# Another order of the first units in a recurrence-and-MLP kernel: unit 1's first scan directly behind its gates, weight conversions and weight sums at other places

## The chip, the cores and the metric

The kernel runs on one core of a Trainium2 chip. The metric is the device time of an execution in microseconds (us). A profiled execution has a span, from its first to its last instruction, and a time that is a little longer than the span.

## The reference

Two blocks follow each other. The first is a recurrence over 768 tokens, for 4 batches and 8 heads of width 48, with a gate for every channel; the second normalises the result and passes it through an MLP with a residual.

```python
f = 1.0 / (1.0 + np.exp(-f_logit))
for t in range(S):
    state = f[:, :, t, :, None] * state + np.einsum('bhd,bhe->bhde', k[:, :, t], v[:, :, t])
    y[:, :, t] = np.einsum('bhd,bhde->bhe', q[:, :, t], state)
...
xn = (x - mu) / np.sqrt(var + 1e-06) * g_ln
ch = np.maximum(xn @ w_ch1, 0.0) @ w_ch2
return x + ch
```

Here x is y with its heads side by side (384 columns), w_ch1 is 384 x 1536 and w_ch2 is 1536 x 384. The weights come as 64-bit floating-point numbers; the kernel computes in 32 bits.

## The kernel before

The 768 tokens are cut into 12 units of 64 tokens, each with all 4 batches. A unit passes through two chains of stages.

The first is the attention of unit n, written `a{n}.stage`. `gates` transposes f_logit on TensorE (only in units 0 to 2; later units get their transposed inputs by DMA) and takes the sigmoid on ScalarE. `after` and `upto` are two scans on VectorE, the products of gates behind and up to each token (lines 669 and 681). `kx` transposes k, and `k` and `q` multiply k and q by the scans. `scores` multiplies q and k on TensorE into the PSUM tile `shared`, and `causal` masks the product on VectorE. `carried` (with the state of the unit before) and `values` fill the tile `py`. `kt` transposes k back, `chunk` and `state` bring the state forward, with `kept` in between. `stats` are means and variances (VectorE, and for `rstd` GpSimd), `norm` makes xn, and `turn` transposes xn to xt on TensorE and ScalarE. In unit 0 most stages are done in two halves, whose names end in 0 and 1.

The second chain is the MLP, `m{n}`: a step is one group of matmuls. `ph` is the first layer with a relu on ScalarE, `po` and `pp` are the second. For unit 0 the first layer is done in halves by the steps `h00` and `h01` (line 901); unit 1 and unit 2 use line 1023, and from unit 3 on the first layer works with fewer products on sums of weights (the tiles `v`, line 612), and from unit 2 on the second layer does so too (the tiles `mixed`, line 586).

The weights come in 12 pieces of 768 KB. `f` fetches a piece, `r` reads it on ScalarE (two conversions, `upper` and `units`), `w` writes it (three VectorE operations, the first on `body`, the last on `upper`, and one addition on GpSimd, line 563). `u` and `U` make one of the sums of w1 on VectorE or GpSimd, `t` and `T` four differences of w2. `l` and `L` load an input of a unit on SP's or ScalarE's DMA queue (`l2f` is f_logit of unit 2, a last digit is a half); `p`, `P` and `x` split an input into planes (a copy on ScalarE), write them out on GpSimd's or SP's queue, and read them back transposed. `d` is a matmul whose result nobody uses, and which only keeps TensorE busy.

Nothing schedules this work at run time or at build time. The first units stand in a list of such words, START, and the rest in a list UNIT, repeated for each unit. The function `run` takes a list word by word, and each word writes its instructions at the end of the queues of its engines; an engine takes its queue in order. The tile framework adds the waits. PSUM has four single banks that are used in rotation (`one_bank`), so a matmul group also waits until the reader of the group four before it is done.

```python
            elif kind in "lL":
                queues = (nc.scalar if kind == "L" else nc.sync,)
...
                {"r": read, "w": write, "f": fetch, "t": mix, "d": idle,
                 "T": lambda: mix(nc.gpsimd), "u": mix_step,
                 "U": lambda: mix_step(nc.gpsimd)}[token]()
```

Of the kernel before, what the change touches and what calls it, by code (L numbers as in the profile page):

```python
# [299 lines left out]


START = """
l0q0 L0f1 d d a0.carried d a0.gates0 d a0.after0 l0k0 a0.upto0 f a0.q0 a0.gates1 a0.kx0 l0k1 r
l0q1 a0.after1 f a0.kx1 a0.k0 a0.scores0 a0.upto1 w L0v1 a0.causal0 a0.k1 l0v0 a0.q1 r f
a0.scores1 a0.values0 r w f a0.kt a0.causal1 l1f a0.stats0 d w a0.values1 l1q a0.norm0 r d
a0.chunk a0.turn0 f a0.stats1 w a1.gates h00 h00 a0.norm1 f a0.turn1 r a1.after h00 a0.state
l2f h01 a1.upto w l1k h01 a1.kept f h01 h01 h00 a2.gates a1.q a1.kx a1.carried r l1v a1.k w f
a1.scores l3f a1.causal h00 r h01 a1.values a1.kt l2k f l2q w a1.stats r h01 a1.norm a1.chunk
P3f0 w h00 a1.turn a2.kx a2.after p3f1 a2.k r m1 m1 a2.upto f f l3k w a2.q r p3k0 x3f a1.state
m1 f a2.kept l4v P3k1 l2v m1 l3q r m1 m1 w x3k r a2.carried a3.gates w a2.scores w u U  # L310
a2.causal P3q1 m0 m0 a2.kt a3.after m0 U P3q0 L4f a2.values a3.k a2.stats L4k a2.chunk P4f1 m1
x3q m1 a2.state a3.upto p4f0 m0 l5f a2.norm U p3K1 u m0 a2.turn m0 P4k0 m1 P3K0 T a3.q x4f u u
P4k1 u a4.gates l4q u a3.kt a3.kept m2 m2 P5f0 m2 a3.carried l3v a4.after a3.scores m2 p4q0 x4k
m2 a4.upto u m2 u a3.causal p4q1 t m2 s2 a3.chunk a4.k t L5k a3.values a3.state x4q p5k0
a3.stats m1 m1 a3.norm P5f1 P4K1 m2 U m2 a4.q x5f m2 p5k1 l6f l5q m2 a4.kept m2 a3.turn y3 l5v
U m2 m1 p4K0 a5.gates
"""
UNIT = """
a{n}.kt a{n}.carried p{p}f1 a{o}.after a{n}.scores m{m} a{n}.causal m{m} m{m} m{m} P{o}q0 m{m}
# [874 lines left out]
```

## Time and profile before

| | |
|---|---|
| median of 3 runs | 430.95 us (430.91 to 432.98) |
| profiled execution | 431.19 us, span 429.4 us |
| mean granted clock of TensorE | 0.987 of full speed |
| TensorE (PE) busy | 414.6 us, 97% of the span |
| VectorE (DVE) busy | 335.2 us, 78% |
| ScalarE (ACT) busy | 214.2 us, 50% |
| GpSimd (POOL) busy | 120.7 us, 28% |

Each engine has one queue, and an engine is busy while it runs an instruction. Where one engine is busy all the time, the others matter only where it waits for them. The lines of the page and of the timelines are read in the prediction.

### The profile page before, as it was taken

To read this page: it belongs to the slowest core of one execution; us is meant where nothing else is said; L and a number is where in the kernel's file an instruction comes from. 1 tells how busy PE (TensorE), PEld (TensorE's weight loads), DVE (VectorE), ACT (ScalarE), POOL (GpSimd) and SP (SyncE) were. 2 spreads that over 40 slices of the span, in tenths; PEclk is the share of its full clock that TensorE was granted. 3 is DMA by queue.
4 is the path that set the end of the run, shared out by engine and by line. 5 is a ranking of instruction groups with operands and counts; after the bars stand their busy time and mean duration, and the time that the engine had idled before them with its cause. 6 is when DMAs were issued, how large, how long until landed. Compare 5 with 4: busy or idle time off the path is not lost.

```text
span 429.4 us, 12958 instructions
## 1 busy us (share of the span) xinstructions
PE 414.6 (97%) x5429; PEld 386.7 (90%) x5429; DVE 335.2 (78%) x539; ACT 214.2 (50%) x364; POOL 120.7 (28%) x148
## 2 busy tenths in 40 slices
PE   5699999999999999999999999999999999999995
PEld 3589988657879899999999999999999999999995
DVE  5998797795886779879879879879879879665561
ACT  2485856542553473573574573574574462351320
POOL 2362453561024116016016016016015014012021
PEclk9599999999999999999999999999999999999999
DMA  9998979886988797896898797797796781301001
GB/s 170 287 226 182 241 237 215 187 212 178 178 134 227 169 215 190 201 207 174 200 186 202 193 217 170 186 213 196 176 209 166 175 135 44 94 2 25 15 9 34
DMA packets 167647, 71.68 MB, mean 167 GB/s; under 512 B 151760, under 2 KB 157840, under 8 KB 167584
## 3 DMA queue, kind: packets, MB, share of 16 engines
q1 hardware_dynamic: 151728, 54.38, 60.1%
q0 software_dynamic: 3872, 12.64, 8.3%
q10 hardware_dynamic: 11984, 3.79, 4.2%
q8 instruction: 44, 0.72, 0.7%
q14 instruction: 19, 0.16, 0.1%
HBM read 28.31 MB, written 23.59 MB: 121 GB/s over the span
## 4 chain that ended last, share of the span: by engine, by line
PE 88%; ACT 3%; DVE 2%; SPq 2%; DMA 2%; issue 1%; POOL 0%; ACTq 0%; DVEq 0%; POOLq 0%
PE pp L1052 32%; PE bx L952 11%; PE by L952 10%; PE ph L1023 7%; PE po L1033 5%; PE bz L952 4%; PE ph L901 3%; PE py L808 2%; PE py L758 2%; PE shared L772 2%; PE bw L952 2%; PE bv L952 2%; SPq L475 2%; PE xp L887 2%; PE shared L846 2%; DMA kraw<-in_k_dram 1%
## 5 line engine op out<-in xcount | busy, mean ns | idle before, releaser
L963 ACT ACTIVATE h<-h 128x512 f32<-128x512 f32 x45 | 28.4, 630 | 44.1 <-DVE h L960 37.9
L1052 PE MATMUL pp<-mixed,h 128*128 128x192 f32 x240 | 42.4, 326 | 0.0
L1052 PE MATMUL pp<-w,h 128*128 128x192 f32 x240 | 40.8, 326 | 0.0
L1052 PE MATMUL pp<-mixed,s 128*128 128x192 f32 x240 | 40.6, 326 | 0.0
L1052 PEld LDWEIGHTS pp<-mixed,s 128*128 128x128 f32 x240 | 39.3, 190 | 0.0
L1052 PEld LDWEIGHTS pp<-w,h 128*128 128x128 f32 x240 | 38.9, 190 | 0.3
L1052 PEld LDWEIGHTS pp<-mixed,h 128*128 128x128 f32 x240 | 39.1, 190 | 0.1
L960 DVE TENSOR_TENSOR h<-h,bx 128x512 f32<-128x512 f32 x36 | 24.6, 683 | 17.1 <-PE bx L952 16.4
L889 ACT ACTIVATE xt<-xp,gain 128x128 f32<-128x128 f32 x72 | 20.0, 376 | 34.5 <-PE xp L887 34.5
L669 DVE TENSOR_TENSOR_SCAN after<-gates,ends 128x1040 f32<-128x1040 f32 (+1 forms) x13 | 29.8, 2290 | 6.0 <-ACT gates L700 3.2
L440 ACT COPY Kplanes<-kh 128x1024 uint16<-128x1024 uint16 x18 | 18.2, 1047 | 29.0 <-DVE kh L717 25.2
L441 POOL DMA_DIRECT2D qhalves<-qplanes x9 | 4.9, 545 | 98.4 <-ACT qplanes L440 98.4
L1033 PE MATMUL po<-w,h 128*128 128x384 f32 x96 | 32.3, 489 | 0.0
L1023 PE MATMUL ph<-xt,w 128*128 128x256 f32 x144 | 31.9, 380 | 0.2 <-ACT xt L889 0.2
L1023 PEld LDWEIGHTS ph<-xt,w 128*128 128x128 f32 x144 | 27.1, 190 | 4.3 <-ACT xt L889 0.5
L952 PE MATMUL bx<-y,v 128*128 128x128 f32 x216 | 28.7, 275 | 0.1
L681 DVE TENSOR_TENSOR_SCAN upto<-gates,starts 128x1040 f32<-128x1040 f32 (+1 forms) x13 | 28.1, 2158 | 0.5
L1033 PEld LDWEIGHTS po<-w,h 128*128 128x128 f32 x96 | 17.8, 190 | 11.3
L952 PEld LDWEIGHTS bx<-y,v 128*128 128x128 f32 x216 | 26.4, 192 | 0.1
L834 POOL TENSOR_SCALAR rstd<-mv 128x2 f32<-128x2 f32 (+1 forms) x13 | 8.1, 626 | 62.2 <-DVE mv L832 61.9
L440 ACT COPY kplanes<-kraw 128x1024 uint16<-128x1024 uint16 x18 | 18.3, 1047 | 9.1 <-DMA kraw<-in_k_dram 6.0
L563 POOL TENSOR_TENSOR w<-w_0upper,w_0units 128x768 int32<-128x768 int32 x7 | 14.6, 2082 | 28.6 <-DVE w_0upper L561 28.6
(172 smaller groups left out, 960.5 us busy)
## 6 DMA issues: line engine op xcount, KB each, us to landing
w_0words<-in_moe_w_ch_dram SPq DMA_DIRECT2D x7, 768.0 KB, 5.0
v<-in_v_dram SPq DMA_DIRECT2D x46, 96.0 KB, 4.0
Khalves<-Kplanes POOLq DMA_DIRECT2D x16, 256.0 KB, 3.6
kraw<-in_k_dram SPq DMA_DIRECT2D x40, 96.0 KB, 4.2
fhalves<-fplanes POOLq DMA_DIRECT2D x14, 256.0 KB, 3.8
kraw<-in_q_dram SPq DMA_DIRECT2D x36, 96.0 KB, 3.0
fraw<-in_f_logit_dram ACTq DMA_DIRECT2D x27, 96.0 KB, 3.0
khalves<-kplanes POOLq DMA_DIRECT2D x9, 256.0 KB, 3.6
```

The source lines that it names most:

```text
L440: nc.scalar.copy(out=to, in_=src)
L563: nc.gpsimd.tensor_tensor(out=to.bitcast(I32), in0=upper, in1=units, op=ALU.add)
L669: nc.vector.tensor_tensor_scan(out=at["after"].rearrange(flat)[:, c0:c1][:, ::-1], data0=gt[:, c0 + 1:c1 + 1][:, ::-1], data1=ends.rearran ...
L681: nc.vector.tensor_tensor_scan(out=at["upto"].rearrange(flat)[:, c0:c1], data0=gt[:, c0:c1], data1=starts.rearrange(flat)[:, c0:c1], initi ...
L889: nc.scalar.mul(out=xt[:, m, g * P:(g + 1) * P], in_=pt[:, m], mul=gain[:, m:m + 1])
L901: nc.tensor.matmul(ph[:, j], lhsT=w1[:, m, (i + j) * P:(i + j + 1) * P], rhs=xt[:, m, tokens], start=m == 0, stop=m == KD - 1)
L952: nc.tensor.matmul(banks[bank][:, i], lhsT=right[:, i * P:(i + 1) * P], rhs=left, start=new and i == 0, stop=True, skip_group_check=True)
L960: nc.vector.tensor_tensor(out=out[to], in0=out[to], in1=bank, op=op)
L963: nc.scalar.activation(out=out[to], in_=out[to] if bank is None else bank, func=AF.Relu)
L1023: nc.tensor.matmul(ph[:, j], lhsT=w1[:, m, (i + j) * P:(i + j + 1) * P], rhs=xt[:, m], start=m == 0, stop=m == KD - 1)
L1033: nc.tensor.matmul(po, lhsT=h[:, i, g * P:(g + 1) * P], rhs=w2[:, i], start=i == 0, stop=i == KF - 1)
L1052: nc.tensor.matmul(pp, lhsT=a[:, i], rhs=b[:, i], start=i == 0, stop=i == KH - 1)
```

## The change

Only START changes. It holds the same number of words before and after, 243, and the same stages and steps of the MLP. GpSimd makes one sum of w1 more than before, and VectorE one less. The other words of the table read like the lines shown. Of the loads and the writes of planes, several change their queue: `l0f1` and `l0v1`, halves of unit 0's f and v, go from ScalarE's queue to SP's; `L2f`, `L3q`, `L3v`, `L4q`, `L4v`, `L5v` and `L6f` come to ScalarE's from SP's, and `l4f` leaves it. The rest is order.

```diff
 START = """
...
-a0.chunk a0.turn0 f a0.stats1 w a1.gates h00 h00 a0.norm1 f a0.turn1 r a1.after h00 a0.state
-l2f h01 a1.upto w l1k h01 a1.kept f h01 h01 h00 a2.gates a1.q a1.kx a1.carried r l1v a1.k w f
...
+a0.chunk a0.state a0.turn0 a0.norm1 a1.gates a1.after r l1k w L2f h00 a1.upto h00 a0.turn1 r h00 f
+w h01 h01 a2.gates h01 a1.kept h01 h00 f l1v a1.q a1.kx r a1.k a1.carried a1.scores a1.causal w l3f
...
```

The queues show what the words do. In all of these pieces the names are those of the tiles, with their running numbers; the line numbers are one lower in the changed kernel.

The first instructions of TensorE before, from the first idle matmuls to the first values of unit 0 (py); tr are transposes, shared the scores:

```order
L577 MATMUL idle<-ident 128x256 x3
L661 MATMUL tr_138<-ident,fraw 128x128 x4
L577 MATMUL idle<-ident 128x256
L661 MATMUL tr_155<-ident,qraw 128x128 x4
L661 MATMUL tr_162<-ident,fraw 128x128 x4
L661 MATMUL tr_168<-ident,kraw 128x128 x4
L661 MATMUL tr_184<-ident,kraw 128x128 x4
L772 MATMUL shared<-qh_154,kh_189 64x64 x16
L661 MATMUL tr_223<-ident,qraw 128x128 x4
L772 MATMUL shared<-qh_154,kh_189 64x64 x16
L808 MATMUL py_132<-v_215,sc_218 64x48 x16
```

TensorE at the same place in the changed kernel:

```order
L576 MATMUL idle<-ident 128x256 x2
L660 MATMUL tr_136<-ident,fraw 128x128 x4
L660 MATMUL tr_151<-ident,qraw 128x128 x4
L660 MATMUL tr_158<-ident,fraw 128x128 x4
L660 MATMUL tr_166<-ident,kraw 128x128 x4
L660 MATMUL tr_175<-ident,kraw 128x128 x4
L576 MATMUL idle<-ident 128x256 x2
L660 MATMUL tr_209<-ident,qraw 128x128 x4
L771 MATMUL shared<-qh_150,kh_190 64x64 x16
L576 MATMUL idle<-ident 128x256 x2
L807 MATMUL py_130<-v_187,sc_236 64x48 x16
L771 MATMUL shared<-qh_150,kh_190 64x64 x16
```

Two idle matmuls instead of three stand ahead of the first transpose, the four others stand in pairs behind the transposes of k and behind the first scores (before, one stood behind the first transposes and two behind the second scores), and the first values come ahead of the second scores.

VectorE from the first xn of unit 0 to the second scan of unit 1, before; xn is norm, and after and upto are the scans:

```order
L876 TENSOR_SCALAR xn_338<-x_268,mv_302,rstd_303 128x384
L831 BN_STATS stats_301<-x_268 128x6
L832 BN_AGGR mv_302<-stats_301 128x2
L556 TENSOR_SCALAR w_768body<-w_768upper 128x768
L559 TENSOR_SCALAR w_768body<-w_768body 128x768
L561 SCALAR_TENSOR_TENSOR w_768upper<-w_768upper,w_768body 128x768
L876 TENSOR_SCALAR xn_338<-x_268,mv_302,rstd_303 128x384
L669 SCALAR_TENSOR_TENSOR after_397<-gates,ends 128x1040
L678 TENSOR_SCALAR total_399<-after_397 128x16
L680 RECIPROCAL starts<-total_399 128x16
L681 SCALAR_TENSOR_TENSOR upto_398<-gates,starts 128x1040
```

VectorE at the same place in the changed kernel:

```order
L875 TENSOR_SCALAR xn_338<-x_261,mv_290,rstd_291 128x384
L830 BN_STATS stats_289<-x_261 128x6
L831 BN_AGGR mv_290<-stats_289 128x2
L875 TENSOR_SCALAR xn_338<-x_261,mv_290,rstd_291 128x384
L668 SCALAR_TENSOR_TENSOR after_390<-gates,ends 128x1040
L555 TENSOR_SCALAR w_768body<-w_768upper 128x768
L558 TENSOR_SCALAR w_768body<-w_768body 128x768
L560 SCALAR_TENSOR_TENSOR w_768upper<-w_768upper,w_768body 128x768
L677 TENSOR_SCALAR total_392<-after_390 128x16
L679 RECIPROCAL starts<-total_392 128x16
L680 SCALAR_TENSOR_TENSOR upto_391<-gates,starts 128x1040
```

The write of the piece w_768 has moved from ahead of the second xn to between the two scans. (The scans are named SCALAR_TENSOR_TENSOR here and TENSOR_TENSOR_SCAN in the profile.) Farther on, unit 1's mask product has moved ahead of the write of w_1280.

ScalarE from the first xt (turn of unit 0) to the second, before; h are the relus of ph:

```order
L547 ACTIVATE w_768upper<-w_768words 128x768
L548 ACTIVATE w_768units<-w_768words 128x768
L889 ACTIVATE xt_378<-xp_379,gain 128x128 x3
L700 ACTIVATE gates<-tr_400 128x8x64
L700 ACTIVATE gates<-tr_406 128x8x64
L903 ACTIVATE h_412<-ph_413 128x2x128
L903 ACTIVATE h_412<-ph_421 128x2x128
L889 ACTIVATE xt_378<-xp_432,gain 128x128 x3
```

ScalarE at the same place in the changed kernel, with the copy of unit 0's state ahead, which before stood behind the second xt:

```order
L855 COPY state<-shared 128x768
L888 ACTIVATE xt_381<-xp_382,gain 128x128 x3
L699 ACTIVATE gates<-tr_393 128x8x64
L699 ACTIVATE gates<-tr_399 128x8x64
L546 ACTIVATE w_768upper<-w_768words 128x768
L547 ACTIVATE w_768units<-w_768words 128x768
L474 DMA fraw<-in_f_logit_dram 64x8x48 x4
L902 ACTIVATE h_423<-ph_424 128x2x128
L902 ACTIVATE h_423<-ph_435 128x2x128
L888 ACTIVATE xt_381<-xp_443,gain 128x128 x3
```

The two conversions of w_768 stand behind unit 1's gates, and the four loads of unit 2's f stand between them and the relus.

More of the change, by code (lines that the diff above doesn't have):

```diff
@@ L302 @@
 START = """
-l0q0 L0f1 d d a0.carried d a0.gates0 d a0.after0 l0k0 a0.upto0 f a0.q0 a0.gates1 a0.kx0 l0k1 r
-l0q1 a0.after1 f a0.kx1 a0.k0 a0.scores0 a0.upto1 w L0v1 a0.causal0 a0.k1 l0v0 a0.q1 r f
-a0.scores1 a0.values0 r w f a0.kt a0.causal1 l1f a0.stats0 d w a0.values1 l1q a0.norm0 r d
-a0.chunk a0.turn0 f a0.stats1 w a1.gates h00 h00 a0.norm1 f a0.turn1 r a1.after h00 a0.state
-l2f h01 a1.upto w l1k h01 a1.kept f h01 h01 h00 a2.gates a1.q a1.kx a1.carried r l1v a1.k w f
-a1.scores l3f a1.causal h00 r h01 a1.values a1.kt l2k f l2q w a1.stats r h01 a1.norm a1.chunk
@@ L309 @@
[L309 to L314, printed above, removed]
@@ L315 @@
-a3.stats m1 m1 a3.norm P5f1 P4K1 m2 U m2 a4.q x5f m2 p5k1 l6f l5q m2 a4.kept m2 a3.turn y3 l5v
-U m2 m1 p4K0 a5.gates
+d d l0q0 a0.carried l0f1 a0.gates0 a0.after0 a0.upto0 l0k0 f a0.q0 a0.gates1 l0k1 a0.kx0 r a0.kx1
+a0.after1 l0q1 d f l0v0 a0.k0 d a0.upto1 r w f a0.k1 a0.q1 a0.scores0 d l0v1 a0.causal0 w d
+a0.values0 r l1f a0.scores1 a0.stats0 a0.causal1 a0.kt f w a0.values1 f a0.norm0 l1q a0.stats1
+a0.chunk a0.state a0.turn0 a0.norm1 a1.gates a1.after r l1k w L2f h00 a1.upto h00 a0.turn1 r h00 f
@@ new lines @@
+w h01 h01 a2.gates h01 a1.kept h01 h00 f l1v a1.q a1.kx r a1.k a1.carried a1.scores a1.causal w l3f
+f h00 a1.values a1.kt l2k a1.stats a1.norm p3f0 h01 r w l2q a1.chunk h01 h00 a1.turn r l2v f r
+a2.kx a2.after a2.k m1 w f l3k p3f1 m1 a1.state w a2.upto p3k0 r a2.kept w m1 f P3k1 m1 m1 m1 r f w
+x3f m1 L3q T a2.q P3q1 p3q0 m0 a2.carried a2.scores m0 r w m1 L4v l4f P4f1 a2.causal a3.gates a2.kt
+a2.values a3.after x3k a2.chunk a2.state p4f0 L4k L3v a2.stats t l5f m0 p4k0 p5f0 a2.norm x3q m0
+p4k1 m0 m0 a2.turn a3.k m1 p3K1 m2 p3K0 m2 a3.upto a3.kept a3.q x4f u u U U u u U u U L4q m2 p4q0
@@ L317 @@
+p4q1 a3.carried a4.gates a3.scores m2 a3.causal L5k U a4.after m2 a3.kt U m1 x4k p5f1 t p5k0 a4.k
+P4K1 P4K0 m2 s2 x4q m2 a3.values a3.stats a4.upto L6f a3.chunk m2 m2 a3.norm m2 a4.q x5f m1
+a3.state u a3.turn a5.gates m2 y3 u a4.kept P5k1 l5q m2 m2 m1 L5v
 """
```

## The prediction

> **What bounds the kernel now.** I read the page first (engines, then the chain that ended last), then the share of TensorE by stretch, then the timelines of the first 60 us.
>
> ```profile
> PE 414.6 (97%) x5429; PEld 386.7 (90%) x5429; DVE 335.2 (78%) x539; ACT 214.2 (50%) x364; POOL 120.7 (28%) x148
> PE 88%; ACT 3%; DVE 2%; SPq 2%; DMA 2%; issue 1%; POOL 0%; ACTq 0%; DVEq 0%; POOLq 0%
> 0.00:26.29 26.29, 16.97 (x248) 0.81 1.02 213
> 26.29:100.00 73.71, 72.66 (x871) 1.00 0.88 213
> 100.00:420.00 320.00, 319.95 (x4283) 1.00 0.69 156
> ```
>
> The last three rows give a stretch, its length, TensorE's busy time, its granted clock, the DMA share and GB/s. From 100 to 420 us TensorE is never idle (0.05 us). The change moves work and takes none of it away, so it can win only what TensorE waits before 100 us: 9.3 us up to the first matmul of the MLP at 26.29, and 1.05 us from there to 100. It can lose by making new waits, at any place up to about 160 us.
>
> The first 42 us are a chain through VectorE (DVE), with GpSimd (POOL) and ScalarE (ACT) in it:
>
> ```profile
> 2.17 2.93 PE L577 MATMUL idle<-ident 128*128 128x256 f32 x6 [2.17 <-POOL ident masks.py:199]
> L661 PEld LDWEIGHTS tr<-ident,fraw x8: 138/163/226, 4.6 to 7.8; 128*128 128x128 f32 x8
> 5.10 0.69 PE tr L661 x4
> 18.80 0.96 DVE L561 SCALAR_TENSOR_TENSOR w_256upper<-w_256upper,w_256body 128x768 int32<-128x768 int32 x1
> 19.68 0.68 DVE L784 TENSOR_TENSOR sc<-shared,causal 128x512 f32<-128x512 f32 x1
> 20.58 0.56 DVE L831 BATCH_NORM_STATS2 stats<-x 128x6 f32<-128x384 f32 x1 [0.22 <-ACT x L819]
> 21.52 0.63 DVE L556 TENSOR_SCALAR w_512body<-w_512upper 128x768 f32<-128x768 f32 x1 [0.16 <-ACT w_512upper L547]
> 23.72 0.48 DVE L876 TENSOR_SCALAR xn<-x,mv,rstd 128x384 f32<-128x384 f32 x1
> 27.82 0.47 DVE L876 TENSOR_SCALAR xn<-x,mv,rstd 128x384 f32<-128x384 f32 x1
> 28.21 3.94 DVE L669 TENSOR_TENSOR_SCAN after<-gates,ends 128x1040 f32<-128x1040 f32 x1
> 32.68 2.33 DVE L681 TENSOR_TENSOR_SCAN upto<-gates,starts 128x1040 f32<-128x1040 f32 x1
> 34.92 0.54 DVE L556 TENSOR_SCALAR w_1024body<-w_1024upper 128x768 f32<-128x768 f32 x1
> 36.96 0.95 DVE L739 TENSOR_TENSOR kept<-state,total 128x768 f32<-128x768 f32 x1
> 38.92 1.29 DVE L688 TENSOR_TENSOR qh<-tr,upto 128x512 f32<-128x512 f32 x2 [1.01 <-PE tr L661]
> 40.20 1.28 DVE L688 TENSOR_TENSOR kh<-tr,after 128x512 f32<-128x512 f32 x2
> 43.53 1.22 DVE L778 TENSOR_TENSOR sc<-shared,causal 128x1024 f32<-128x1024 f32 x1
> 19.91 1.82 POOL L563 TENSOR_TENSOR w<-w_256upper,w_256units 128x768 int32<-128x768 int32 x1 [2.23 <-DVE w_256upper L561]
> 26.48 0.87 POOL L835 TENSOR_TENSOR rstd<-rstd,power 128x1 f32<-128x1 f32 x1
> 28.04 1.92 POOL L563 TENSOR_TENSOR w<-w_768upper,w_768units 128x768 int32<-128x768 int32 x1 [0.70 <-DVE w_768upper L561]
> ```
>
> Start, length, engine, line, operation; in brackets the idle time ahead and what ended it. Two things are to be seen. Unit 1's first scan (28.21) took 3.94 us, while the other full scan (32.68) took 2.33: GpSimd's addition of a weight piece had begun 0.17 us ahead of it, and 28.04 + 1.92 + 2.33 is 32.3, where the slow scan ended. And from 34.92 on VectorE has 1.01 us to spare: qh waits there for TensorE.
>
> **The change part by part.** All times below are mine, from these rows.
>
> *Start of unit 0.* Two fillers instead of three stand ahead of the first transpose. Three take 2.93 us, so one is 0.98; the gates' data was there by 4.6, when its weight load began, and the transpose ran at 5.10. Gain 0.5 us, and VectorE, which works without a gap from 6.5 to 19.7, carries it on: the piece w_256 is written by 19.26.
>
> *Two swaps on VectorE.* The first statistics now stand ahead of the second mask product: that product ends at 19.26 + 0.56 + 0.18 + 0.68 = 20.7 (before 20.36). Piece w_512 can start there instead of at 21.52, but GpSimd's addition of w_256 now lies at 19.4 to 21.2 and holds its first instruction, as it held the scan; it ends about 23.3 (before 23.8). The first xn comes at 23.2 instead of 23.72.
>
> *First matmul of the MLP.* Before, a conversion stood between the turned xn and TensorE; now it stands behind unit 1's gates:
>
> ```profile
> 24.13 0.94 ACT L547 ACTIVATE w_768upper<-w_768words 128x768 f32<-128x768 f32 x1
> 25.78 0.87 ACT L889 ACTIVATE xt<-xp,gain 128x128 f32<-128x128 f32 x3
> 26.29 2.92 PE L901 MATMUL ph<-xt,w 128*128 128x128 f32 x24 [0.44 <-ACT xt L889]
> 29.37 8.20 PE L901 MATMUL ph<-xt,w 128*128 128x128 f32 x72
> 37.41 1.04 PE L661 MATMUL tr<-ident,fraw 128*128 128x128 f32 x8
> 42.20 0.68 PE L772 MATMUL shared<-qh,kh 48*64 48x64 f32 x28 [0.32 <-issue]
> 45.69 1.15 PE L808 MATMUL py<-v,sc 64*64 64x48 f32 x64
> 10.72 1.29 ACTq L475 DMA_DIRECT2D v<-in_v_dram  x2
> 26.38 4.14 SPq L475 DMA_DIRECT2D fraw<-in_f_logit_dram  x4
> ```
>
> Turning at 23.7, eight transposes of unit 1's f behind it (about 0.9), so ph starts at 24.95, 1.3 us earlier. A group of ph (x12) is 1.35 us.
>
> *Unit 1's first scan.* The second rstd follows GpSimd's addition of w_512 (23.4 to 25.3) and takes 0.42 + 0.87, as at 26.48: xn at 26.65, while VectorE waits 2 us. The scan starts at 27.1 (before 28.21) and has no addition beside it: 2.33 us, done at 29.4 instead of 32.15. But the piece w_768 (2.05 us) now stands behind it, and its addition falls at 31.6, just ahead of the second scan, which takes over the wait: 33.5 + 2.33 = 35.8, against 35.0 before. With w_1024 and kept (3.0) qh starts at 38.8 and kh ends at 41.35. Of the 2.75 us that the first scan gains, 0.1 is left at qh. The added wait could also be nothing (34.3) if the addition came second; I take 35.8, the row it is nearest to.
>
> *Loads on ScalarE's queue.* The four loads of unit 2's f go from SP to ACT, ahead of the ph evictions. Four cost 2 x 1.29 = 2.6 us by the nearest ACT row, 4.14 by the row of the same loads on SP; nothing, if they are issued while older work runs. I take 2.6, the same queue: from about 27.0 to 29.6, then two evictions and xt, so the third-next group waits until 30.7; TensorE is there at 29.4. Wait 1.3 us. From 30.7: two groups, eight transposes, three groups, 16 transposes, reach 40.1 at 1.35 and 0.9; carried 1.0; the scores wait for kh and end at 42.1 (before 42.88).
>
> *Unit 1's mask product* stands directly behind kh, where a piece (2.1 us) stood before, and one group instead of two covers it: values at 43.5, with one group fewer done. Before, 45.69 - 1.35 = 44.34. **Gain to here: 0.8 us.** The product itself, 42.1 + 1.22 = 43.3, is just covered.
>
> *Later.* Two waits are left in the stretch to 100 us:
>
> ```profile
> 53.65 5.45 PE L1023 MATMUL ph<-xt,w 128*128 128x256 f32 x24 [0.23 <-ACT xt L889]
> 82.71 1.06 PE L846 MATMUL shared<-v,kt 64*48 64x48 f32 x64 [0.46 <-ACT kt L801]
> 120.07 4.00 ACTq L475 DMA_DIRECT2D kraw<-in_k_dram  x4
> ```
>
> The first stays, its order is the same. For the second, q's planes, which held the copies of kt, are now copied before the scores; 0.3 of 0.46 goes. Sums of w2 and w1 move between VectorE and GpSimd, hidden behind 2.7 us groups of po (75 to 100 us, VectorE and GpSimd both idle in part); bounds 0 to 1.3 us, one blocked addition of the kind above, taken as 0. Loads moved to ACT further on (q3, v4, v3, q4, f6, v5) lie behind four PSUM banks of work; 0 taken, up to 4.0 each as a bound.
>
> Sum: -0.8 - 0.3 = -1.1. The profiled execution was 431.19 us (span 429.4), which gives 430.1. The median of the runs is 430.95, 0.24 lower: **429.9 us**.
>
> **A rule weighed.** Rows: granted clock, by stretch.
>
> ```profile
> 11.00:14.00 3.00, 2.19 (x39) 0.71 1.15 287
> 14.00:17.00 3.00, 0.56 (x3) 0.50 1.31 204
> 17.00:20.00 3.00, 2.44 (x67) 0.50 1.03 365
> 22.00:24.00 2.00, 2.00 (x71) 0.87 0.87 116
> ```
>
> TensorE went to half clock at about 12.3 us (0.71 is the mean of 11 to 14), after idling, was busy again from about 17.5, and had full clock back at about 22.5 (0.87 over 22 to 24), after some 5 us. The Trainium skill ("TensorE: Matmul & The Clock Gate", Part 1) says that a window of about 3.4 us decides, an idle one for half, a busy one for full clock; the trace agrees in kind. By it the change's four fillers at 12 to 17 us would restore the clock early, and a quieter stretch before ph could lose it again.
>
> **The rivals.**
> *A, the queue (slower).* The four loads cost ACT the 4.14 us of the SP row, DMA being full then (0.88 to 1.02 busy). The group then starts at 32.25, values at 45.05: 0.7 us lost, with 0.3 won later 431.4. Above an issue time of 3.7 us (2.6 and the 1.1 of the sum) the change is slower than before. For it: ACT is in order, and at 120.07 four loads held it 4.00 us. Against: the ACT row of 1.29. The same block at a later load could add up to 2 us more.
> *B, the whole gain.* GpSimd's addition does not come ahead of the second scan, and the issues hide behind ACT's older work. Then kh ends at 40.4, scores at 41.05, values at 42.4: 1.9 us, and all of 0.46: 428.6. For it: an addition that comes second waits instead. Against: two short instructions stand between piece and scan, time enough for the addition.
> *C, the clock.* VectorE and GpSimd now hold TensorE nearly idle from 17.5 to 24; if it loses its clock there, ph runs at half from 24.95 for the 5 us that the rows show, and loses 2.5, of which 1.3 was waiting anyway: 1.2 later than forecast, 431.1, no change. If the clock comes back early instead, nothing is won: VectorE, not TensorE, sets 17 to 27 us.
>
> **How the numbers follow.** Chances: forecast 0.43 (its own range 428.9 to 430.9), A 0.23, B 0.21, C 0.13. 0.5% is 2.15 us, about what a measurement of this kernel tells from no change: below 428.8 is faster, above 433.1 slower. Most of B and a little of the forecast are faster: 0.22. A third of A, with a second blocked load, and a remainder are slower: 0.12. The rest, 0.66, is no change. The range takes B with no loss elsewhere and A with a second block: 427.4 to 433.2.
>
> **What would show it.** Right: first ph at about 25; unit 1's first scan near 2.3 us from about 27 and the second near 3.9; values at 43.5 with nine groups of ph done. A: ACT's issue of fraw longer than 3.7 us, with ph waiting on an eviction or xt. B: both scans at 2.3. C: a granted clock of 0.5 after 24 us. The prediction is wrong if TensorE waits anew between 60 and 160 us for ACT, a load, or a weight sum; it is nearly never idle there now.

## The result: slower, and the profile after

The changed kernel takes 446.06 us (median of 4 runs, 444.22 to 447.79), the kernel before 431.41 beside it: a ratio of 1.033, 95% interval 1.027 to 1.040. That is 14.6 us more, where 429.9 was forecast. The profiled execution took 444.44 us.

The page of the changed kernel, busy time of the engines and the chain that ended last:

```profile
PE 419.4 (95%) x5429; PEld 390.2 (88%) x5429; DVE 333.1 (75%) x537; ACT 215.1 (49%) x364; POOL 129.1 (29%) x155
PE 76%; DMA 7%; DVE 6%; ACT 3%; issue 3%; POOL 2%; SPq 2%; ACTq 0%; DVEq 0%; POOLq 0%
```

TensorE's share of the chain fell from 88 to 76%, and loads are in it with 7% (before 2%). To find the place, cut both executions at the same two instructions, the first matmul of the MLP and the scores of unit 4. Before, by stretch (columns: stretch, length, TensorE busy, its granted clock, DMA share, GB/s):

```profile
0.00:26.29 26.29, 16.97 (x248) 0.81 1.02 213
26.29:143.14 116.85, 115.80 (x1378) 1.00 0.88 204
143.14:429.40 286.26, 281.82 (x3818) 1.00 0.65 148
```

After:

```profile
0.00:28.09 28.09, 18.47 (x248) 0.94 0.96 215
28.09:155.13 127.04, 119.13 (x1378) 0.96 0.81 182
155.13:442.70 287.57, 281.85 (x3818) 1.00 0.65 148
```

The same 1378 matmuls in the middle take 10.2 of the 13.3 us of span: 6.9 more of waiting (7.91 against 1.05) and 3.3 more of busy time, where the granted clock was at half. The front adds 1.8, the rest 1.3; of that, 0.9 lies behind the last matmul, where the last results go out (5.27 us from there to the end of the span, before 4.39).

The front, timelines of the changed kernel:

```profile
4.75 1.09 PE L660 MATMUL tr<-ident,fraw 128*128 128x128 f32 x4 [0.50 <-DMA fraw<-in_f_logit_dram]
13.83 1.09 PE L660 MATMUL tr<-ident,kraw 128*128 128x128 f32 x4 [3.81 <-DMA kraw<-in_k_dram]
20.18 0.96 DVE L560 SCALAR_TENSOR_TENSOR w_256upper<-w_256upper,w_256body 128x768 int32<-128x768 int32 x1
28.09 4.51 PE L900 MATMUL ph<-xt,w 128*128 128x128 f32 x24
28.96 2.33 DVE L668 TENSOR_TENSOR_SCAN after<-gates,ends 128x1040 f32<-128x1040 f32 x1 [0.22 <-ACT gates L699]
28.51 0.63 ACTq L474 DMA_DIRECT2D fraw<-in_f_logit_dram  x1
30.75 1.29 ACTq L474 DMA_DIRECT2D fraw<-in_f_logit_dram  x2
33.74 3.74 DVE L680 TENSOR_TENSOR_SCAN upto<-gates,starts 128x1040 f32<-128x1040 f32 x1
47.10 1.15 PE L807 MATMUL py<-v,sc 64*64 64x48 f32 x64
```

Seen here: the second half of k is transposed only at 13.83; the piece w_256 ends at 21.14; 24 matmuls of the first ph take 4.51 us instead of 2.92; the two scans are 2.33 and 3.74.

The main stall, from 82 to 94 us, in the timelines of the changed kernel (ScalarE's order, then VectorE, TensorE, SP's queue):

```profile
81.35 1.05 ACT L439 COPY qplanes<-kraw 128x1024 uint16<-128x1024 uint16 x1 [6.78 <-DMA kraw<-in_q_dram]
83.25 0.90 ACT L546 ACTIVATE w_0upper<-w_0words 128x768 f32<-128x768 f32 x1
90.30 1.04 ACT L439 COPY fplanes<-fraw 128x1024 uint16<-128x1024 uint16 x1 [5.34 <-DMA fraw<-in_f_logit_dram]
91.25 1.05 ACT L695 ACTIVATE gates<-turned 128x1024 f32<-128x1024 f32 x1
92.21 1.05 ACT L800 COPY kt<-kp 128x512 f32<-128x512 f32 x2
84.19 0.56 DVE L555 TENSOR_SCALAR w_0body<-w_0upper 128x768 f32<-128x768 f32 x1 [5.83 <-ACT w_0upper L546]
86.32 1.22 DVE L777 TENSOR_TENSOR sc<-shared,causal 128x1024 f32<-128x1024 f32 x1
87.59 1.15 PE L807 MATMUL py<-v,sc 64*64 64x48 f32 x64 [1.25 <-DVE sc L777]
92.83 1.53 PE L845 MATMUL shared<-v,kt 64*48 64x48 f32 x64 [4.09 <-ACT kt L800]
94.29 11.63 PE L1032 MATMUL po<-w,h 128*128 128x384 f32 x32
82.83 2.42 SPq L474 DMA_DIRECT2D fraw<-in_f_logit_dram  x4
```

The same steps before:

```profile
75.23 1.04 ACT L696 ACTIVATE gates<-turned 128x1024 f32<-128x1024 f32 x1
81.13 1.04 ACT L440 COPY qplanes<-kraw 128x1024 uint16<-128x1024 uint16 x1 [4.85 <-DMA kraw<-in_q_dram]
82.08 0.58 ACT L801 COPY kt<-kp 128x512 f32<-128x512 f32 x1
88.36 1.99 ACT L440 COPY fplanes<-fraw 128x1024 uint16<-128x1024 uint16 x2 [2.52 <-DMA kraw<-in_k_dram]
83.70 10.59 PE L1033 MATMUL po<-w,h 128*128 128x384 f32 x32
```

ScalarE waits for unit 3's q until 81 us in both. What differs is what stands behind the wait. Before, the last piece of w and unit 3's gates are done, and kt follows one copy. After, the last piece of w, the planes of unit 4's f (a second wait, for a load that SP issues only behind the write of q's planes) and the gates come first, and kt is copied ten microseconds later, at 92.21. TensorE had transposed kt's blocks by 86.3. VectorE has its own link: unit 2's mask product (sc) stands behind the write of that piece, which waits for ScalarE.

A third place, later, of the same make: the relu that the sums of h need stands behind copies of unit 4's scanned k (timelines of the changed kernel):

```profile
132.88 1.04 ACT L439 COPY Kplanes<-kh 128x1024 uint16<-128x1024 uint16 x1 [1.52 <-DVE kh L716]
134.78 0.59 ACT L1024 ACTIVATE h<-ph 128x512 f32<-128x512 f32 x1
135.40 0.96 DVE L930 TENSOR_TENSOR s<-h 128x768 f32<-128x768 f32 x1 [2.55 <-ACT h L1024]
137.77 4.14 PE L1051 MATMUL pp<-mixed,s 128*128 128x192 f32 x24 [1.43 <-DVE s L931]
```

Before, TensorE did not wait for these sums:

```profile
128.97 4.06 PE L1052 MATMUL pp<-mixed,s 128*128 128x192 f32 x24
```

### The profile page after: what moved, and what is told of

Read it like the earlier page. It is cut to its first block, busy times and chain, and to the rows that moved or that the text cites. A ratio compares the mean times of both kernels' runs of the same rounds, so it can differ in the third digit from the quotient of the medians.

```text
span 442.7 us, 12961 instructions
## 1 busy us (share of the span) xinstructions
PE 419.4 (95%) x5429; PEld 390.2 (88%) x5429; DVE 333.1 (75%) x537; ACT 215.1 (49%) x364; POOL 129.1 (29%) x155
## 4 chain that ended last, share of the span: by engine, by line
PE 76%; DMA 7%; DVE 6%; ACT 3%; issue 3%; POOL 2%; SPq 2%; ACTq 0%; DVEq 0%; POOLq 0%
PE pp L1051 29%; PE bx L951 11%; PE by L951 9%; PE po L1032 4%; PE bz L951 4%; PE ph L900 3%; PE py L807 2%; PE py L757 2%; PE bw L951 2%; PE shared L771 2%; DMA kraw<-in_k_dram 2%; PE bv L951 2%; PE xp L886 2%; DMA turned<-fhalves 2%; DMA kraw<-in_q_dram 2%
## 5 line engine op out<-in xcount | busy, mean ns | idle before, releaser
L1032 PE MATMUL po<-w,h 128*128 128x384 f32 x96 | 33.5, 500 | 0.0
L680 DVE TENSOR_TENSOR_SCAN upto<-gates,starts 128x1040 f32<-128x1040 f32 (+1 forms) x13 | 30.8, 2372 | 0.4
L439 ACT COPY qplanes<-kraw 128x1024 uint16<-128x1024 uint16 x18 | 18.5, 1040 | 12.2 <-DMA kraw<-in_q_dram 12.2
```

What stands on the lines that cost most here:

```text
L439: nc.scalar.copy(out=to, in_=src)
L680: nc.vector.tensor_tensor_scan(out=at["upto"].rearrange(flat)[:, c0:c1], data0=gt[:, c0:c1], data1=starts.rearrange(flat)[:, c0:c1], initi ...
L1032: nc.tensor.matmul(po, lhsT=h[:, i, g * P:(g + 1) * P], rhs=w2[:, i], start=i == 0, stop=i == KF - 1)
```

## The experiments

Three theories at first. Theory 1: ScalarE's order in units 2 to 4. Theory 2: the issue of loads on ScalarE's queue (rival A, at the later places). Theory 3: the front and its clock, which everything later follows. All ratios are to the kernel before, run on the same chip, with 95% intervals.

**Which half.** The two orders have done the same steps after 87 words of START, just behind unit 1's mask product, and can be joined there.

```diff
 front_only: START = first 87 words of the changed table + the rest of the table before
 rest_only:  START = first 87 words of the table before + the rest of the changed table
```

> The changed order up to unit 1's mask product (the first 87 steps), then the order of before. Theory 1 (order further on: most of the loss lies behind ScalarE's and VectorE's queues between 70 and 145 us, and the front costs 2.6): 431.2 + 2.6 = about 434, first matmul of the MLP at half clock near 28.1 us. Theory 2 (the loads moved to ScalarE's queue cost by themselves): the front holds one of them, L2f, so about the same, 433 to 434. Theory 3 (the front and its clock set everything, the later waits follow from it): 440 or more.

> The order of before up to unit 1's mask product, then the changed order. Theory 1: 444.4 - 2.6 = about 442, with the waits at values (1.25 us), chunk (4.1 us) and in 133 to 145 us (2.5 us) all there. Theory 2: about the same. Theory 3: near 432, the later waits gone with the front.

front_only took 435.13 us, 1.004 (1.001 to 1.008): about 2 us. rest_only took 445.72 us, 1.034 (1.027 to 1.041), all of the loss. The two don't add: with the rest in place the front makes no difference to the median. Theory 3 falls, since TensorE still waits 3.96 us for kt in rest_only; theory 1's subtraction of 2.6 was a miss. The profiles show part of the reason: in rest_only the product with kt starts 1.5 us earlier than in the changed kernel (91.34 for 92.83) and the last matmul ends 1.1 us earlier (436.36 for 437.43), but then 6.74 us pass to the end of the span instead of 5.27.

**Queue or order.** mid_order moves kt and the mask product ahead of q's planes, the last piece of w and f4's planes; queues changes letters only; order_fixed moves more; order_and_queues is both.

```diff
-a2.q P3q1 p3q0 m0 a2.carried a2.scores m0 r w m1 L4v l4f P4f1 a2.causal a3.gates a2.kt a2.values
+a2.q m0 a2.carried a2.scores m0 a2.kt a2.causal P3q1 p3q0 r w m1 L4v l4f P4f1 a3.gates a2.values
 queues: L3q L4v l4f L3v L4q L6f L5v -> l3q l4v L4f l3v l4q l6f l5v, at their places
 order_fixed, from a2.kt on:
+a2.kt a2.causal r w a3.gates a3.after P3q1 p3q0 m1 L4v l4f a2.values P4f1
```

> The changed kernel with three steps put in another place in unit 2: the transposes and copies of kt and the mask product come ahead of q's planes, the conversion of the last piece of w, the load of v4 and f4 and unit 3's gates. All queues stay as changed. Theory 1: the waits of 1.25 us at values and 4.1 us at chunk go, and with them the half clock behind them (1 us): 444.4 - 6 = about 438. Theory 2: the issues still hold ScalarE, so 443 to 445. Theory 3: no change, 444.

> The changed order with seven loads behind unit 1's mask product put back on the queue they had before (q3, v4, v3, q4, f6, v5 on SP, f4 on ScalarE). Theory 1: the waits for the data stay, since the copies of q's planes still stand ahead of kt: 441 to 446. Theory 2: the loads' issue on ScalarE was the cost, so 436 to 438. Theory 3: 444.

> As mid_order, and in the same place the last piece of w and unit 3's gates and first scan also come ahead of q's planes, and f4's planes behind unit 2's values. Queues as changed. Theory 1 (ScalarE's order: gates3 stood behind f4's planes and so behind a load that is itself issued behind q3): the wait for the piece of w (1.75 us) and for xn (2.47) of mid_order go; 443.0 - 4 = about 439, and 437 if the block of v3 is hidden too. Theory 2 (ScalarE's queue: the 8.2 us that v3's issue held ScalarE from 98 to 106 us in mid_order): that block stays, TensorE waits for xt or h behind it, 441 to 444.

> As order_fixed, with the seven later loads back on their queues of before (as in the kernel called queues). Theory 1: the same as order_fixed, within 1 us. Theory 2: no block of 8 us on ScalarE, so 3 to 4 us faster than order_fixed, about 436.

Measured: mid_order 443.29 us, 1.029 (1.021 to 1.038); queues 446.94, 1.035 (1.027 to 1.043); order_fixed 445.47, 1.029 (1.022 to 1.036); order_and_queues 446.86, 1.035 (1.030 to 1.041). Theory 2 found no gain from the queues; but theory 1's numbers (438 and 439) failed too: the waits at 87 and 92 us went and others came, in mid_order 1.7 us for the last piece of w, 2.5 for xn and 2.0 for xt. Timelines of order_fixed:

```profile
98.05 10.27 ACTq L474 DMA_DIRECT2D v<-in_v_dram  x4
111.26 1.65 ACT L888 ACTIVATE xt<-xp,gain 128x128 f32<-128x128 f32 x6
112.45 9.59 PE L1022 MATMUL ph<-xt,w 128*128 128x256 f32 x36 [7.49 <-ACT xt L888]
```

And of order_and_queues:

```profile
107.64 1.04 ACT L439 COPY fplanes<-fraw 128x1024 uint16<-128x1024 uint16 x1 [4.73 <-DMA fraw<-in_f_logit_dram]
109.53 1.65 ACT L888 ACTIVATE xt<-xp,gain 128x128 f32<-128x128 f32 x6
110.72 9.70 PE L1022 MATMUL ph<-xt,w 128*128 128x256 f32 x36 [7.48 <-ACT xt L888]
```

The same wait of 7.5 us for unit 2's turned xn, once behind ScalarE's issue of v3 (10.27 us), once, with v3 on SP, behind a copy of unit 5's planes that waits for its load. So neither theory was general enough: whatever holds ScalarE ahead of a step of the current unit costs, be it a wait for a load or a long issue. In the changed order the copies of k4's and f5's planes stand ahead of that xt (`p4k0 p5f0 a2.norm x3q m0 p4k1 m0 m0 a2.turn`); before, they stand behind the turn.

**The copies of planes.** First the reverse test, in the kernel before: three words moved the way of the change, ahead of the copies of kt. They are the second copy of q3's planes, the load of f4 and the first copy of its planes.

```diff
 planes_early (from the table before):
-a2.causal P3q1 m0 m0 a2.kt a3.after m0 U P3q0 L4f a2.values a3.k a2.stats L4k a2.chunk P4f1 m1
+a2.causal P3q1 P3q0 L4f P4f1 m0 m0 a2.kt a3.after m0 U a2.values a3.k a2.stats L4k a2.chunk m1
```

> The kernel before with one step moved the way of the change: the load of f4 and the first copy of its planes ahead of the transposes and copies of kt in unit 2. No queue is changed. Theory 1: kt waits for f4 to land, 4 to 6 us later than 82.1 us, so chunk waits 3 to 5 us and the kernel takes 434 to 436. Theory 2: no load is put on another queue, so 430.5 to 432.

It took 440.20 us, 1.018 (1.013 to 1.024): 7.9 us from these three words, more than the 434 to 436 expected, with every load on its old queue. Timelines of planes_early:

```profile
89.26 1.04 ACT L440 COPY fplanes<-fraw 128x1024 uint16<-128x1024 uint16 x1 [4.32 <-DMA fraw<-in_f_logit_dram]
90.21 0.58 ACT L801 COPY kt<-kp 128x512 f32<-128x512 f32 x1
90.84 1.53 PE L846 MATMUL shared<-v,kt 64*48 64x48 f32 x64 [7.24 <-ACT kt L801]
```

Then the cure, in the changed kernel: all such copies behind the current unit's steps.

```diff
 planes_late:
-P3q1 p3q0 ... r w m1 L4v l4f P4f1 a2.causal a3.gates a2.kt a2.values a3.after x3k a2.chunk a2.state p4f0 L4k L3v
-a2.stats t l5f m0 p4k0 p5f0 a2.norm x3q m0 p4k1 m0 m0 a2.turn a3.k
+r w a2.kt a2.causal a3.gates a3.after P3q1 p3q0 m1 L4v l4f a2.values x3k a2.chunk a2.state a2.stats P4f1 p4f0 L4k
+t l5f m0 a2.norm x3q m0 m0 m0 a2.turn p4k0 p5f0 L3v p4k1 a3.k
-L4q m2 p4q0 p4q1 a3.carried a4.gates a3.scores m2 a3.causal
+L4q m2 a3.carried a4.gates a3.scores m2 p4q0 a3.causal p4q1
-a4.k P4K1 P4K0 m2 s2 x4q
+a4.k m2 s2 P4K1 P4K0 x4q
 planes_late2, further:
-p5f1 t p5k0 a4.k m2 s2 P4K1 P4K0 x4q m2 a3.values a3.stats
+p5f1 t m2 s2 a4.k x4q m2 a3.values a3.stats p5k0 P4K1 P4K0
 planes_late_queues, late2_queues: the same with the seven letters of queues
 front_before: first 87 words of the table before + the rest of planes_late2
```

> The changed kernel with each copy of planes that waits for a load put behind the step of the current unit that TensorE waits for (q3's behind kt, gates3 and the last piece of w; f4's behind unit 2's values and statistics; k4's, f5's and the load of v3 behind the turned xn; q4's behind gates4; the scanned k of unit 4 behind the sums). Queues as changed. Theory 1 (planes: ScalarE's in-order work waits for a load with TensorE's next operand behind it): TensorE's waits between 60 and 150 us fall from 8 to under 2 us, 444.4 - 8 = 436, and 434 if the clock's window goes with them. Theory 2 (the issues on ScalarE's queue hold it 2 to 10 us each): 439 or more, with waits for xt or h behind q4, v4 and v3.

> As planes_late, with the seven later loads on their queues of before. Theory 1: within 1 us of planes_late. Theory 2: 3 us or more faster than planes_late, 434 to 436.

> As planes_late, and in unit 4 the first copy of k5's planes, the scanned k and its copies also stand behind unit 2's sums and unit 3's values. Queues as changed. Theory 1 (planes): the wait of 8.07 us for a ReLU at 133 us goes, and with it 1.7 us at half clock: 442.7 - 9 = about 433 to 434, which is the front's loss alone (front_only took 435.1). Theory 2 (the loads on ScalarE's queue): new waits take its place, 439 or more.

> As planes_late2, with the seven later loads on their queues of before. Theory 1: within 1 us of planes_late2. Theory 2: 3 us or more faster than it.

> The order of before up to unit 1's mask product, then the rest of planes_late2. Theory 1: no loss is left, 429 to 433. Theory 2: as planes_late2 less 2, or 437 and more.

planes_late took 442.71 us, 1.022 (1.015 to 1.029), and planes_late_queues 442.89, 1.024 (1.018 to 1.030). In planes_late TensorE waits longer than 0.2 us only once between 60 and 125 us (0.43), and unit 3's scores start at 108.39 (before 108.98): up to there the loss was gone. Then one copy that I had left ahead of a relu took most of it back, and the 436 expected was missed (timelines of planes_late):

```profile
131.82 1.04 ACT L439 COPY kplanes<-kraw 128x1024 uint16<-128x1024 uint16 x1 [7.65 <-DMA kraw<-in_k_dram]
132.78 0.59 ACT L1024 ACTIVATE h<-ph 128x512 f32<-128x512 f32 x1
133.42 1.65 PE L1051 MATMUL pp<-w,h 128*128 128x192 f32 x4 [8.07 <-ACT h L1024]
```

In planes_late_queues the wait at this relu is only 2.5 us, but unit 3 starts 5.0 us later: the same time does not mean the same waits. With this copy and unit 4's scanned k moved as well, planes_late2 took 437.51 us, 1.013 (1.010 to 1.016): 8.5 of the 14.6 us are back, by order alone and with every load on its changed queue. That is still short of the 433 to 434 expected. late2_queues took 440.14, 1.017 (1.012 to 1.021): not faster, so theory 2 has no support left as a cause by itself. front_before took 437.31, 1.012 (1.010 to 1.015), which misses theory 1's 429 to 433: the front is not the remainder.

Most of what remains lies between unit 3's and unit 4's first products with the state (carried): planes_late2 takes 38.94 us from one to the other, front_before 39.21, the kernel before 34.15. Between 127 and 142 us planes_late2 waits 0.95 us for the sums of h, 0.54 for an issue, 0.70 for xn and 1.38 for a product's addition, 3.6 together. One more attempt:

```diff
 late3, from front_before:
-p4q1 L5k U a4.after ... p5f1 t m2 s2 a4.k ... P4K0 a4.upto L6f a3.chunk m2 m2 a3.norm m2
+p4q1 U a4.after ... t m2 s2 p5f1 L5k a4.k ... P4K0 a3.chunk m2 m2 a3.norm a4.upto L6f m2
```

> As front_before, with the load of k5 behind unit 2's sums (no issue ahead of the ReLU) and unit 4's second scan behind unit 3's normalization. If those two steps are the remainder, the 3.6 us of waits between 127 and 141 us go: 437.3 - 3.6 = about 433.7, with only the 1.0 us at unit 1's values left. If the loads' volume or lateness is it, the waits move elsewhere: 436 or more.

437.86 us, 1.011 (1.006 to 1.016): no gain, a miss. Timelines of late3:

```profile
131.49 5.22 ACTq L475 DMA_DIRECT2D fraw<-in_f_logit_dram  x2
136.76 1.66 ACT L889 ACTIVATE xt<-xp,gain 128x128 f32<-128x128 f32 x6 [4.35 <-DMA Khalves<-Kplanes]
137.39 3.90 PE L1052 MATMUL pp<-mixed,h 128*128 128x192 f32 x12 [2.37 <-DVE p L1060]
```

The waits went to other steps: f6's issue now holds ScalarE ahead of xt, and the moved scan (134.77 to 137.09) holds the addition that frees a bank. In this stretch unit 4's gates start at 115.87 in planes_late2 and at 107.48 before, so more of unit 4 falls into it; whether that is the cause of the last 5 to 6 us was not tried and stays open.

**The front.** scan_alone does the titular part by itself in the kernel before; warm adds idle matmuls to the changed kernel; front_f1 puts two loads of front_only back.

```diff
 scan_alone (from the table before):
-a0.stats1 w a1.gates h00 h00 a0.norm1 f a0.turn1 r a1.after h00 a0.state
+a0.stats1 a0.norm1 a1.gates a1.after w h00 h00 f a0.turn1 r h00 a0.state
 warm: eleven words d between a0.causal0 and a0.turn0
 front_f1: front_only with l0f1, l0v1 -> L0f1, L0v1
```

> The kernel before with one part of the change: unit 1's gates and first scan directly behind the normalization, ahead of the conversion of w_768 on VectorE and GpSimd. Theory 1: the scan takes 2.33 us instead of 3.94, and the time of before changes by less than 1 us (430 to 432.5), since the conversion is only pushed behind it. Theory 'order of the front': the conversion then comes late for the second scan and the time rises by 2 us or more.

> The changed kernel with eleven more idle matmuls between 17 and 25 us, to keep TensorE's clock. Theory 'clock' (the front's loss is the half clock from 24.7 to 31.6 us): the first matmuls of the MLP at 2.9 us for 24 instead of 4.5, and 1.5 to 2.5 us less in all, if the later waits don't take it back: 442 to 443. Theory 'data' (the front is set by the late load of k and VectorE, the clock's loss was waiting anyway): 444 to 445.

> As front_only (435.1), with the second half of f0 and of v0 loaded on ScalarE's queue as before. Theory 'queue of the front' (the half of f0 on SP pushed k's second half and the first piece of w back by 2 us): k's half lands near 11.8 instead of 13.7, the MLP starts near 26.3, and the kernel takes 431.5 to 433. Theory 'VectorE' (VectorE's chain sets the front): 434 to 435.

scan_alone: 433.00 us, 1.002 (0.999 to 1.005), no change. Timeline of VectorE in scan_alone:

```profile
27.89 2.33 DVE L669 TENSOR_TENSOR_SCAN after<-gates,ends 128x1040 f32<-128x1040 f32 x1 [0.33 <-ACT gates L700]
32.66 3.73 DVE L681 TENSOR_TENSOR_SCAN upto<-gates,starts 128x1040 f32<-128x1040 f32 x1
```

The first scan is 1.6 us shorter, the second 1.4 longer. warm: 446.30 us, 1.034 (1.028 to 1.039). The first ph ran at full clock, and unit 1's values came 0.3 us earlier than in the changed kernel (47.10). Timeline of warm:

```profile
29.00 2.84 PE L901 MATMUL ph<-xt,w 128*128 128x128 f32 x24
46.78 1.15 PE L808 MATMUL py<-v,sc 64*64 64x48 f32 x64
```

front_only has the front of the changed kernel, and there too the first 24 matmuls ran at full clock (2.87 us from 27.90); the values came at 46.91. So full clock at ph brings the values at most 0.3 us: the half clock was spent in time that TensorE would have waited anyway. front_f1: 434.53 us, 1.006 (1.003 to 1.010): k's second half was transposed at 11.83 instead of 13.67 in front_only, as expected, but the time did not follow. It lies in the 434 to 435 of theory 'VectorE', which no run tests by itself, so what makes the front 2 us slower is not settled.

## Why the prediction was wrong, point by point

*Later* is the step that failed. It read the order right (q's planes now come ahead) and drew the wrong sign from it: 0.3 of the 0.46 us wait at kt was to go. Measured: 4.09 at kt and 1.25 at the values, so +4.9 in place of -0.3, and some 2 more at 133 to 138 us. I asked which copies had stood ahead of kt, and not what each copy waits for: q's planes wait for a load until 81 us, and f4's, which had come ahead as well, until 90. The table was compared at the front only, where the title pointed; the rest, which by itself costs the whole 14 us (rest_only), was priced in one short paragraph.

*Loads moved to ScalarE further on*, 0 taken with 4.0 each as a bound: right that the queue was not the cause (queues, late2_queues), for a wrong reason. It had PSUM's four banks cover an issue, but in order_fixed one issue held ScalarE 10.27 us, and behind it TensorE waited 7.49 for xt. The issue alone does not explain the 7.49, since in order_and_queues a late load took its place. The Trainium skill ("DMA: Bandwidth & Descriptors", Issuing engines are not separate DMA queues) says that transfers from all engines share the same 16 DMA engines, and that another issuing engine saves only the time of the issue. That agrees with queues, at 446.94 us beside 446.06.

*Start of unit 0*, gain 0.5 carried on: failed. By the timelines the first transposes started 0.14 us earlier (4.75 for 4.89), after 0.50 us of waiting for f, and the four took 1.09 us instead of 0.88, so the first gates came no earlier (5.94 for 5.88). The halves of f and v on SP's queue pushed k's second half back by 2 us, as front_f1 shows; w_256 was written by 21.14, not 19.26. Each queue that a load moves onto should have been followed there. *Two swaps on VectorE* inherited that delay: the first xn came at 25.09 instead of 23.2.

*The two scans*: right. 2.33 and 3.74 for 2.33 and 3.9 said, and scan_alone shows the exchange alone.

*L2f on ScalarE's queue*: 2.6 taken, 3.5 measured (28.51 to 32.04), between forecast and rival A. It was covered: TensorE finished its first two groups at 32.60 and did not wait, nor did it in warm, where they ran at full clock.

*First ph and values*: 28.09 and 47.10 for 24.95 and 43.5, with the nine groups that were said.

*Rival C* came in as a mechanism, half clock at ph; half clock came again with the stall of 4.09 us. By stretches of the changed kernel, with the busy time of each engine (TensorE, its weight loads, VectorE, ScalarE, GpSimd), then the clock:

```profile
25.00:32.00 7.00, 6.29 (x32) 6.32 (x33) 4.70 (x8) 4.44 (x8) 2.73 (x3) 0.53 1.01 203
89.00:97.00 8.00, 4.17 (x69) 2.96 (x70) 4.59 (x7) 5.34 (x8) 0.60 (x2) 0.57 0.76 160
```

The first cost nothing that warm could win back; the second goes with the stall and costs about 1 us in the po groups behind it (11.63 for 32 matmuls, before 10.59). What the text named as its own refutation, TensorE waiting anew between 60 and 160 us for ScalarE or a load, is what came. The range missed because it held at most 2 us for a blocked load later on, and no rival had several such places in series, each hiding the next.

## What to carry to other kernels

When an order is changed by a table, list for every in-order engine the instructions that wait for a load, and look at what stands behind each: a copy for a later unit ahead of an operand of the current one can cost the load's whole remaining flight, however little the copy itself takes. Undo such waits all together, or the next one in the queue takes the time: no partial cure here came below a ratio of 1.022 (the change 1.033), the fuller one 1.013. And compare the whole table, not the part that the title names.

## What the runs showed of the hardware

Four loads of 96 KB took ScalarE's queue between 2 us (k4 in planes_late, 91.57 to 93.56) and 10.27 us (v3 in order_fixed), and what stood behind them on ScalarE started only when they were out (108.42 in order_fixed, after 108.32); the profile put that idle time down to other releasers, in the changed kernel to an output's transfer (7.13 us ahead of 102.82). What stands ahead of an issue need not be done: in the changed kernel L2f's issue began at 28.51, while the two conversions ahead of it in the queue started at 28.83 and 29.62. The clock column can be blind at the start: with the changed start, four transposes took 1.06 to 1.09 us each time up to about 17 us, where before they took 0.63 from 6.7 us on, and where the column gives 0.50 before, four took 1.11 (at 13.45). By these durations TensorE ran at about half clock, while the column shows 1.00 up to 24 us; presumably it shows full clock as long as no change has been recorded.
